# Moving fourteen subtractions from GpSimd to VectorE in a fused attention and Mish kernel, with a new written order for its four blocks

## The chip, the cores and the metric

One core of a Trainium2 chip runs the kernel in one launch. The metric is device time in microseconds (us); the time before is the median of three runs. A core has TensorE (PE in the profile: matrix products into PSUM), VectorE (DVE), ScalarE (ACT), GpSimd (POOL), and a queue on SyncE (SP) from which nearly all DMAs of this kernel are issued, in order. The engines run on their own and wait for each other through semaphores.

## The reference, cut to what matters

Two branches read the same `x` of 2048 x 512 and a gate mixes them.

```
qkv = x @ wqkv                              # 32 heads of 16
pq, pk = q @ w_phi[h], k @ w_phi[h]
phi = concat(softmax(p), softmax(-p))       # for q and for k: 32 features a head
kv  = phi_k^T v ;  z = sum_s phi_k
o   = (phi_q kv) / (phi_q z + 1e-6)
a   = o @ wo
h   = x @ w1 + b1                           # 512 -> 1376
act = h * tanh(log(1 + exp(h)))             # Mish
b   = act @ w2
g   = sigmoid(sum(x * gate_w))
out = g * a + (1 - g) * b
```

## The kernel before

**Two phases.** Phase A goes over 8 chunks of 256 rows (keys `("A", c)`) and makes keys, values, `phi_k^T v`, `z` and the queries' projection `pq`, which goes to DRAM as `pqd`. Phase B goes over 4 blocks of 512 rows, B0 to B3 (keys `("B", b)`). Each block does the Mish branch for its rows, and the softmax work of the queries, `num` (`phi_q kv`) and the product with `wo`. All matmuls run on fp32r operands: an fp32 value is split into a high part (`act(h, x)`, a copy on ScalarE that rounds) and a low part (`l = x - h`, a subtraction on VectorE or GpSimd), and a product is three matmuls (h*h, h*l, l*h). So each operand made on the way costs a copy and a subtraction.

**The order is written by hand.** Each piece of work is a named step, put in a table by `at(key, name, fn)`. `run` walks a text of names and calls them; `'`, `"` and `+` after a name mean the previous block, the one before that, and the next block. Each engine's queue holds the instructions in the order in which the text calls them (`tc.keep_in_program_order`), and SP's DMAs too. BLOCK0 to BLOCK3 are these texts; from B1 on they are built from `pairs(g, ...)`, g = 0 to 3, and `end(...)`.

**Steps of the softmax work, for tile t of 4 (128 rows each) of a block.** `lq` loads `pq` by SP. `mx`, `mn` (VectorE, maximum and minimum per head), `d0`, `d1` (VectorE, the differences for the two signs, into `E`), `E` (ScalarE, Exp), `S` (sum per head), `T` (`E` times `z`), `rS` (reciprocal), `D` (sum of T), `m`, `de`, `rd`, `sc` (small ones on 32 or 64 columns), `es` (`E` times the scale), `tr` (a transpose on VectorE, then an SP DMA to a DRAM tile `ed`). `mv0` and `mv1` are four SP DMAs each, which bring `ed` of tiles 0 and 1, or 2 and 3, back as `eT`. `nu0` and `nu1` are 32 small matmuls each from `eT` into two PSUM banks `num`; `oh` (ScalarE) and `ol` (VectorE) split them into `ohl`, of which there are two buffers in all; `wo0` to `wo3` are 12 matmuls each, `wo0` and `wo1` from `nu0`, `wo2` and `wo3` from `nu1`. `ag` (ScalarE) scales `wo` by the gate into `io`, `fi` (VectorE) adds the Mish branch and sends the tile out. `ge` and `gg` make the gate; `gr` and `gl` move its row through DRAM.

**Steps of the Mish branch.** B0 has 11 column groups: `up` (12 matmuls), `mi` (ScalarE, Mish), `hi` (ScalarE), `lo` (GpSimd, the low part), `dn` (12 matmuls). B1 to B3 have one such group, and five pairs of groups that share seven products of 6 matmuls of 256 columns. Within `pairs(g, ...)` TensorE runs `s3_g`, then `s1` of the next pair, `s4_g`, a `dn`, `s2` of the next pair and a `dn`. VectorE adds partial sums in `a1`, `a2`, `a3` (line 787); `s4_g` overwrites what `a3_g` reads. ScalarE copies in `c1`, `c2` and does Mish in `M0`, `M1` and the high parts in `H0`, `H1`; GpSimd makes the low parts in `L0`, `L1` (line 806). `wa` and `wb` load weight sums (`wA`, `wB`) from a DRAM tile `prod`.

**Steps that prepare the next block.** `LX0`, `LX1` load `xraw` by SP. `XH0`, `XH1` (ScalarE) and `XL0`, `XL1` (line 567; VectorE for B0, GpSimd for the others) make the parts of `x`; `TT0` to `TT3` (VectorE, lines 584 to 588) make differences, which `TH0`, `TH1` (ScalarE) and `TL0`, `TL1` (GpSimd, line 601) split. `ls`, `hs`, `os`, `ts` (line 493 is `os`) load weight sums, split them and send them to `prod`; `ldo`, `WH`, `WL` (line 627 is `WL`) do so with `wo`, and `wh0`, `wl0` in B0 with the last piece of `w2b` (line 437 is `wl`).

ScalarE holds one table of functions at a time. Exp and Mish are in different ones; a load stands in its queue wherever the next function needs the other.

Of the kernel before, what the change touches and what calls it, by code (L numbers as in the profile page):

```python
# [107 lines left out]
BLOCK3 = (
    """
    up0 mi0 S0 T0 s1_0 wb_0 c1_0 hi0 a1_0 lo0 gr df2' fi2' df3' fi3' gl s2_0 c2_0 a2_0 M0_0 H0_0 L0_0 hc rS0 D0 m0 de0 rd0 sc0 dn0  # L110
    """
    + pairs(0, "es0", "tr0 S1 T1", "rS1 D1 m1 de1 rd1 sc1")
    + pairs(1, "es1", "tr1 mv0 S2 T2", "rS2 D2 m2 de2 rd2 sc2")
    + pairs(2, "es2", "tr2 S3 T3", "ge rS3 D3 m3 de3 rd3 sc3")
    + pairs(3, "es3", "gg tr3 mv1", "cd nu0 oh0 ol0")
    + """
    s3_4 wa_4 a3_4 wo0 ag0 s4_4 wb_5 M1_4 H1_4 L1_4 wo1 ag1 nu1 oh1 ol1 df0 fi0 df1 fi1 wo2 ag2 wo3 ag3 mo df2 fi2 df3 fi3
    """
# [4 lines left out]
def tile_gated_mix(ctx: ExitStack, tc: tile.TileContext, xT, wv, wkT, wqT, bd, w1a, w1b, b1, w2a, w2b, wo, out):  # L123
# [328 lines left out]
    def sum_ops():  # L452
# [25 lines left out]
        for g in range(NFB):  # L478
# [10 lines left out]
            def hs(d=d):  # L489
                act(d["h"], f32(d["l"]))  # L490

            def os(d=d):
                pin(G_.tensor_sub(d["l"], f32(d["l"]), f32(d["h"])))
# [58 lines left out]
    def x_ops(b, load, split):  # L552

        raw = {}
        for h in range(2):
# [8 lines left out]

            def xl(h=h):
                sl = slice(h * SC, (h + 1) * SC)
                pin((G_ if b else V).tensor_sub(xb[b][1][:, :, sl], kt(raw[h], SC), f32(xb[b][0][:, :, sl])))
# [587 lines left out]
```

## Time and profile before

| | |
|---|---|
| median of three runs (459.22 to 463.14) | 460.75 us |
| time of the profiled execution | 464.13 us |
| its span, first to last instruction | 462.4 us |
| phase A on TensorE | until about 150 us |
| B0, up to the first matmul of B1 | 150 to 237.94 us |
| B1 | 237.94 to 308.88 us |
| B2 | 308.88 to 385.96 us |
| B3 and the end | 385.96 to 462.4 us |
| busy: TensorE, VectorE, ScalarE, GpSimd | 96%, 77%, 49%, 45% |

The profile is one execution. Its views are: the page (shares, the span in 40 slices, the costliest groups), the waits of an engine (who waited for whom), the timeline of an engine (start, length, engine, line, operation, output and inputs; in brackets the idle time before it and what ended that), windows (busy time in a stretch) and groups by line. "SPq" rows are DMA issues on SyncE's queue. A matmul's length in the timeline overlaps its successor's; the distance of their starts is what it takes. Lines are those of the kernel before.

### The profile page before, as it was taken

Reading aid. Unit: us, or ns where it says so; the run is one execution under the profiler, and the core shown is the slowest. Engines: PE = TensorE matmul, PEld = TensorE weight load, DVE = VectorE, ACT = ScalarE, POOL = GpSimd, SP = SyncE. Lnnn points to the kernel's source line nnn. Section 1 sums busy time; section 2 is a strip of 40 time slices with the busy share of each in tenths; the row PEclk is TensorE's granted clock in tenths of the full one; section 3 lists DMA queues with packets and bytes.
Section 4 is the critical chain, followed back from the end, with each engine's and each line's share of the span. In section 5 each row is a group of like instructions: output and inputs, shape, how many; then the busy total and the mean of one; then the engine's idle time right before and its main releaser. Section 6 shows DMA issues by size and latency. Waiting matters only on the chain.

```text
span 462.4 us, 7984 instructions
## 1 busy us (share of the span) xinstructions
PE 443.3 (96%) x3144; PEld 371.7 (80%) x3144; DVE 354.1 (77%) x471; ACT 228.5 (49%) x355; POOL 206.6 (45%) x121
## 2 busy tenths in 40 slices
PE   8999999999999989996699999999999969999997
PEld 7888888888888868783488988878899748888876
DVE  3996937858799999996985897646897588899522
ACT  3644434434425356554538634488333668544631
POOL 3078795896364274551743422462222182222210
PEclk9999999999999999998889999999999989999999
DMA  8721989998531348819849967715889831867512
GB/s 257 268 92 50 324 241 231 257 349 278 176 119 64 86 121 322 229 52 317 315 183 296 368 258 233 307 45 190 291 229 321 239 123 55 286 221 219 196 49 92
DMA packets 53214, 96.50 MB, mean 209 GB/s; under 512 B 6836, under 2 KB 27828, under 8 KB 53176
## 3 DMA queue, kind: packets, MB, share of 16 engines
q1 hardware_dynamic: 51640, 91.00, 58.6%
q0 software_dynamic: 1248, 4.59, 5.2%
q8 instruction: 25, 0.41, 0.4%
q10 hardware_dynamic: 288, 0.39, 0.3%
q14 instruction: 13, 0.11, 0.1%
HBM read 69.35 MB, written 33.17 MB: 222 GB/s over the span
## 4 chain that ended last, share of the span: by engine, by line
PE 35%; DVE 22%; DMA 6%; ACT 4%; issue 2%; SPq 0%; POOL 0%; DVEq 0%; ACTq 0%
PE down L134 15%; PE upa L134 7%; PE wo L134 7%; PE upb L134 5%; DMA xraw<-in_xT_dram 3%; DVE E L320 2%; DVE T L873 2%; DVE Dn L877 2%; DVE E L303 2%; DVE Sm L309 1%; DVE xt L588 1%; DMA ed<-E 1%; PE up L134 1%; DVE xt L584 1%; DVE E L888 1%
## 5 line engine op out<-in xcount | busy, mean ns | idle before, releaser
L806 POOL TENSOR_TENSOR l<-act,h 128x512 fp32r<-128x512 f32 x30 | 40.8, 1359 | 121.0 <-ACT h L154 84.7
L363 POOL TENSOR_TENSOR zacc<-zacc,E 128x1024 f32<-128x1024 f32 x16 | 39.6, 2477 | 34.5 <-DVE E L320 24.8
L134 PE MATMUL wo<-woh,ohl 128*128 128x512 f32 x128 | 44.7, 417 | 8.1 <-ACT ohl L154 7.9
L154 ACT ACTIVATE E<-E 128x1024 f32<-128x1024 f32 x32 | 33.3, 1058 | 37.8 <-DVE E L305 37.7
L320 DVE TENSOR_TENSOR E<-E,Sm 128x1024 f32<-128x1024 f32 x32 | 48.9, 1530 | 0.7
L309 DVE TENSOR_REDUCE Sm<-E 128x64 f32<-128x1024 f32 x32 | 38.5, 1202 | 1.7 <-ACT E L154 1.7
L716 POOL TENSOR_TENSOR l<-act,h 128x512 fp32r<-128x512 f32 (+1 forms) x14 | 19.4, 1392 | 45.0 <-ACT h L154 20.3
L134 PEld LDWEIGHTS wo<-woh,ohl 128*128 128x128 f32 x128 | 26.0, 203 | 15.0 <-ACT ohl L154 8.7
L134 PE MATMUL down<-w2ah,h 128*128 128x512 f32 x95 | 37.3, 392 | 0.0
L787 DVE TENSOR_TENSOR act<-upb,act 128x256 f32<-128x256 f32 x30 | 12.6, 421 | 28.1 <-ACT act L154 18.9
L134 PE MATMUL down<-w2ah,l 128*128 128x512 f32 x79 | 31.0, 392 | 1.6 <-POOL l L716 1.6
L134 PE MATMUL down<-w2bh,h 128*128 128x512 f32 x79 | 32.1, 407 | 0.0
L154 ACT ACTIVATE h<-act 128x512 fp32r<-128x512 f32 (+2 forms) x48 | 30.3, 632 | 3.1 <-ACT act L154 0.7
L134 PE MATMUL down<-w2bl,h 128*128 128x512 f32 x79 | 31.4, 398 | 0.0
L134 PE MATMUL down<-w2bh,l 128*128 128x512 f32 x79 | 31.0, 393 | 0.0
L134 PE MATMUL down<-w2al,h 128*128 128x512 f32 x79 | 30.9, 392 | 0.0
L289 DVE TENSOR_REDUCE mx<-proj 128x32 f32<-128x512 f32 x16 | 11.0, 689 | 25.3 <-PE proj L134 25.3
L281 POOL TENSOR_TENSOR xl<-xraw,xh 128x512 fp32r<-128x512 f32 x14 | 20.4, 1601 | 18.6 <-ACT xh L154 18.6
L931 DVE TENSOR_TENSOR ohl<-num,ohl 128x512 fp32r<-128x512 f32 x16 | 10.4, 686 | 21.7 <-ACT ohl L154 18.7
L134 PE MATMUL wo<-wol,ohl 128*128 128x512 f32 x64 | 26.8, 419 | 0.0
L154 ACT ACTIVATE qs<-proj 128x512 f32<-128x512 f32 x16 | 9.6, 599 | 33.4 <-PE proj L134 29.1
L154 ACT ACTIVATE act<-act,b1s 128x512 f32<-128x512 f32 (+1 forms) x30 | 18.4, 614 | 13.9 <-DVE act L787 13.8
(170 smaller groups left out, 1202.2 us busy)
## 6 DMA issues: line engine op xcount, KB each, us to landing
wA<-prod SPq DMA_DIRECT2D x15, 1024.0 KB, 5.8
wB<-prod SPq DMA_DIRECT2D x15, 768.0 KB, 5.7
ed<-E SPq DMA_DIRECT2D x16, 512.0 KB, 4.5
eT<-ed SPq DMA_DIRECT2D x32, 256.0 KB, 4.7
xraw<-in_xT_dram SPq DMA_DIRECT2D x15, 512.0 KB, 7.7
...
```

Source lines behind the costliest of these rows:

```text
L134: return pin(nc.tensor.matmul(*a, **k))
L154: return pin(A_.activation(out_, in_, fn, **k))
L281: pin(eng.tensor_sub(xs[c][1][j], kt(rawx[c], SC)[:, 2 * j : 2 * j + 2, :], f32(xs[c][0][j])))
L289: pin(V.tensor_reduce(d[name], hv(src()), axis=AX.X, op=op))
L303: pin(V.tensor_sub(E, hv(src()), d["mx"][:, :, None].to_broadcast([P, H, DH])))
L309: pin(V.tensor_reduce(d["S"], hv(d["E"][:, :]), axis=AX.X, op=ALU.add))
L320: pin(eng.tensor_mul(hv(d["E"][:, :]), hv(d["E"][:, :]), d["S"][:, :, None].to_broadcast([P, 2 * H, DH])))
L363: at(key, f"z{t}", lambda d=d: pin(G_.tensor_add(zacc, zacc, d["E"])))
L716: pin(G_.tensor_sub(U[i]["l"][:n, :], U[i]["a"][:n, :], f32(U[i]["h"][:n, :])))
L787: pin(V.tensor_add(o, ps, o))
L806: pin(G_.tensor_sub(u["l"], d["A"][j], f32(u["h"][:, :])))
L931: pin(V.tensor_sub(ohl[h, gp][:, 512:], num[h, gp], f32(ohl[h, gp][:, :512])))
```

## The change

Fourteen low parts that GpSimd made are made by VectorE: `wl0` in B0, `os` of all five groups, `WL0` and `WL1`, and `XL0`, `XL1` of B1, B2 and B3. GpSimd keeps `lo`, `L0`, `L1`, `TL0`, `TL1`.

In B0 the whole softmax work of B1's tile 0 and most of tile 1's (`S` to `tr`) leaves the end of the block; only `mx` to `E` of both tiles and `S0`, `T0`, `rS0` stay. In B1 and B2, `mx` to `E` of the next block's tiles 2 and 3 leave the end, except `mx2` and `mn2`, and are done within the next block's pairs 0 and 1. `D0` to `tr0` come after `a3_0`. `nu0` comes before `dn8` in B0, and `nu1` behind `dn9`. `LX0`, `LX1` stand behind `mv1` in each block. In `end`, `oh1` and `ol1` stand ahead of `TT2`, `TT3`, `TH0`, and `XL1` ahead of `TT0`. In B0, `ls2` and the `ts` steps are issued at other places. The step `pm` puts the load of Mish's table directly behind the Exps.

```diff
-    up0 lq3 mi0 gr gl hi0 lo0 ldo0 ldo1 S1 rS1 up1 up2 mi1 hi1 lo1 hs0 os0 wh0 wl0 d02 d12 T0 D0 m0 de0 rd0 sc0 es0 tr0 mi2 hi2 ts0 up3 dn0 hc lo2 hs1 os1
-    mi3 hi3 lo3 T1 D1 m1 de1 rd1 sc1 es1 tr1 ts1 mv0 lq0+ lq1+ mx3 mn3 d03 d13 WH0 dn1
-    up4 mi4 hi4 lo4 WH1 WL0 dn2 E2 S2 T2 rS2 D2 m2 de2 rd2 sc2 es2 tr2 up5 mi5 hi5 lo5 WL1 dn3 E3 ge gg up6 mi6 hi6 lo6 ls2 dn4
-    up7 mi7 hi7 lo7 dn5 S3 T3 rS3 D3 m3 de3 rd3 sc3 es3 tr3 mv1 hs2 os2 up8 mi8 hi8 lo8 dn6
-    mx0+ mn0+ d00+ d10+ mx1+ mn1+ d01+ d11+ lq2+ lq3+ ts2 up9 mi9 hi9 lo9 dn7 E0+ E1+ S0+ T0+ LX0 rS0+ D0+ LX1 m0+ de0+ rd0+ sc0+
-    up10 mi10 hi10 lo10 dn8 dn9 cd nu0 nu1 ls3 wi oh0 XH0+ XH1+ XL0+ XL1+ ol0 TT0+ TT1+ TT2+ TT3+ es0+ tr0+ TH0+ TL0+ TH1+ TL1+ S1+ df0 df1 wo0 ag0
-    wo1 oh1 ol1 T1+ rS1+ ag1 D1+ fi0 m1+ de1+ rd1+ sc1+ hs3 os3 df2 wo2 ag2 fi1 es1+ wo3 ag3 ts3 tr1+ ls4+
+    up0 lq3 mi0 gr gl hi0 lo0 ldo0 ldo1 S1 rS1 up1 up2 mi1 hi1 lo1 wh0 wl0 hs0 d02 d12 T0 D0 m0 de0 rd0 sc0 es0 tr0 mi2 hi2 os0 up3 dn0 hc lo2 hs1
+    mi3 hi3 lo3 T1 D1 m1 de1 rd1 sc1 es1 tr1 ts0 os1 mv0 lq0+ lq1+ mx3 mn3 d03 d13 WH0 dn1
+    up4 mi4 hi4 lo4 WH1 WL0 WL1 ls2 ts1 dn2 E2 pm S2 T2 rS2 D2 m2 de2 rd2 sc2 es2 tr2 up5 mi5 hi5 lo5 dn3 E3 ge pm gg up6 mi6 hi6 lo6 dn4
+    up7 mi7 hi7 lo7 hs2 os2 ts2 dn5 S3 T3 rS3 D3 m3 de3 rd3 sc3 es3 tr3 mv1 up8 mi8 hi8 lo8 dn6
+    mx0+ mn0+ d00+ d10+ mx1+ mn1+ d01+ d11+ lq2+ lq3+ up9 mi9 hi9 lo9 dn7 LX0 LX1
+    up10 mi10 hi10 lo10 E0+ E1+ pm nu0 dn8 oh0 ol0 cd dn9 nu1 ls3 wi XH0+ XH1+ XL0+ XL1+ TT0+ TT1+ df0 df1 wo0 ag0
+    wo1 oh1 ol1 TT2+ TT3+ ag1 TH0+ TL0+ TH1+ TL1+ fi0 hs3 os3 df2 wo2 ag2 fi1 S0+ T0+ rS0+ wo3 ag3 ts3 ls4+
...
-def end(f3, last):
+def end(f3, last, tail):
...
-    s3_4 wa_4 a3_4 wo0 ag0 {f3} s4_4 wb_5 M1_4 H1_4 L1_4 dn9 XH0+ XH1+ XL0+ XL1+ TT0+ TT1+ TT2+ TT3+ wo1 ag1 TH0+ TL0+ nu1 oh1 ol1 TH1+ TL1+ {last} df0 df1 wo2 ag2 wo3 ag3 fi0 fi1
+    s3_4 wa_4 a3_4 wo0 ag0 {f3} s4_4 wb_5 M1_4 H1_4 L1_4 dn9 XH0+ XH1+ XL0+ d01+ d11+ XL1+ TT0+ TT1+ wo1 ag1 nu1 oh1 ol1 TT2+ TT3+ TH0+ TL0+ {tail} TH1+ TL1+ pm {last} df0 df1 wo2 ag2 wo3 ag3 fi0 fi1
...
 BLOCK1 = (
-    up0 mi0 mx2 mn2 hi0 s1_0 wb_0 c1_0 gr a1_0 lo0 mv0 gl fi2' df3' fi3' d02 d12 s2_0 c2_0 a2_0 M0_0 H0_0 L0_0 mx3 mn3 hc dn0
+    up0 mi0 s1_0 wb_0 c1_0 hi0 a1_0 lo0 gr gl fi2' df3' fi3' s2_0 c2_0 a2_0 M0_0 H0_0 L0_0 hc dn0
...
-    + pairs(0, "d03 d13", "lq0+ lq1+ lq2+", "hs4 os4 S2 T2 rS2", "E2 E3 ge")
-    + pairs(1, "D2 m2 de2 rd2 sc2", "es2 tr2", "ts4 S3 T3 rS3 gg")
-    + pairs(2, "D3 m3 de3 rd3 sc3", "es3 tr3 mv1", "mx0+ mn0+ d00+ d10+ lq3+")
-    + pairs(3, "mx1+ mn1+ LX0 LX1", "d01+ d11+ mx2+ mn2+", "cd nu0 oh0 ol0 d02+ d12+")
-    + end("mx3+ mn3+ d03+ d13+", "E0+ E1+ E2+ E3+")
+    + pairs(0, "D0 m0 de0 rd0 sc0", "es0 tr0 mx2 mn2", "os4 d02 d12", "hs4")
+    + pairs(1, "mx3 mn3 d03 d13", "S1 T1 rS1 D1", "m1 de1 rd1 sc1 es1 ts4", "E2 E3 ge pm")
+    + pairs(2, "tr1 mv0", "S2 T2 rS2 D2", "m2 de2 rd2 sc2 es2 tr2 lq0+ lq1+ lq2+")
+    + pairs(3, "S3 T3 rS3", "D3 m3 de3 rd3 sc3 es3 tr3 mv1 LX0 LX1", "mx0+ mn0+ cd nu0 oh0 ol0 gg")
+    + end("d00+ d10+ mx1+ mn1+ lq3+", "mx2+ mn2+", "E0+ E1+")
 BLOCK2 = (
-    up0 mi0 S0 T0 s1_0 wb_0 c1_0 hi0 a1_0 lo0 gr df2' fi2' df3' fi3' gl s2_0 c2_0 a2_0 M0_0 H0_0 L0_0 hc rS0 D0 m0 de0 rd0 sc0 dn0
+    up0 mi0 S0 T0 s1_0 wb_0 c1_0 hi0 a1_0 lo0 gr df2' fi2' df3' fi3' gl s2_0 c2_0 a2_0 M0_0 H0_0 L0_0 hc rS0 dn0
...
-    + pairs(0, "es0", "tr0 S1 T1", "rS1 D1 m1 de1 rd1 sc1 lq0+ lq1+ lq2+")
-    + pairs(1, "es1", "tr1 mv0 S2 T2", "rS2 D2 m2 de2 rd2 sc2")
-    + pairs(2, "es2", "tr2 S3 T3", "rS3 D3 m3 de3 rd3 sc3")
-    + pairs(3, "es3", "tr3 mv1 mx0+ mn0+ LX0 LX1", "d00+ d10+ cd nu0 oh0 ol0 lq3+ ge gg")
-    + end("mx1+ mn1+ d01+ d11+", "mx2+ mn2+ d02+ d12+ mx3+ mn3+ d03+ d13+ E0+ E1+ E2+ E3+")
+    + pairs(0, "D0 m0 de0 rd0 sc0", "es0 tr0 d02 d12", "mx3 mn3 d03 d13")
+    + pairs(1, "S1 T1 rS1", "D1 m1 de1 rd1 sc1 es1 tr1", "", "E2 E3 ge pm")
+    + pairs(2, "mv0 S2 T2", "rS2 D2 m2 de2 rd2 sc2 es2", "lq0+ lq1+ lq2+ tr2 S3 T3")
+    + pairs(3, "rS3 D3 m3 de3 rd3 sc3", "es3 tr3 mv1 LX0 LX1", "mx0+ mn0+ cd nu0 oh0 ol0 gg")
+    + end("d00+ d10+ mx1+ mn1+ lq3+", "mx2+ mn2+", "E0+ E1+")
```

BLOCK3 changes as BLOCK2 does, without what it would prepare for a next block. The rest of the change:

```diff
     def run(text, key, prev=None, nxt=None, prev2=None):
         for w in text.split():
...
+            if w == "pm":
+                pin(A_.preload_act_table_set("mish"))
...
-                pin(G_.tensor_sub(l[:, o : o + n], r, f32(h[:, o : o + n])))
+                pin((V if c == NCH - 1 else G_).tensor_sub(l[:, o : o + n], r, f32(h[:, o : o + n])))
...
-            def os(d=d):
-                pin(G_.tensor_sub(d["l"], f32(d["l"]), f32(d["h"])))
+            def os(d=d, g=g):
+                pin((V if g == 2 else V).tensor_sub(d["l"], f32(d["l"]), f32(d["h"])))
...
-                pin((G_ if b else V).tensor_sub(xb[b][1][:, :, sl], kt(raw[h], SC), f32(xb[b][0][:, :, sl])))
+                pin((V if b else V).tensor_sub(xb[b][1][:, :, sl], kt(raw[h], SC), f32(xb[b][0][:, :, sl])))
...
-            pin(G_.tensor_sub(wob["l"][:, sl], raw[j], f32(wob["h"][:, sl])))
+            pin(V.tensor_sub(wob["l"][:, sl], raw[j], f32(wob["h"][:, sl])))
```

More of the change, by code (lines that the diff above doesn't have):

```diff
@@ L109 @@
     """
-    up0 mi0 S0 T0 s1_0 wb_0 c1_0 hi0 a1_0 lo0 gr df2' fi2' df3' fi3' gl s2_0 c2_0 a2_0 M0_0 H0_0 L0_0 hc rS0 D0 m0 de0 rd0 sc0 dn0
+    up0 mi0 S0 T0 s1_0 wb_0 c1_0 hi0 a1_0 lo0 gr df2' fi2' df3' fi3' gl s2_0 c2_0 a2_0 M0_0 H0_0 L0_0 hc rS0 dn0
     """
[L112 to L115, printed above, removed]
+    + pairs(0, "D0 m0 de0 rd0 sc0", "es0 tr0 d02 d12", "mx3 mn3 d03 d13")
+    + pairs(1, "S1 T1 rS1", "D1 m1 de1 rd1 sc1 es1 tr1", "", "E2 E3 ge pm")
+    + pairs(2, "mv0 S2 T2", "rS2 D2 m2 de2 rd2 sc2 es2", "tr2 S3 T3")
+    + pairs(3, "rS3 D3 m3 de3 rd3 sc3", "es3 tr3 mv1", "cd nu0 oh0 ol0 gg")
     + """
```

## The prediction

> **What bounds the kernel now.** I read the page first, then TensorE's waits, then its timeline row by row, then windows of VectorE's load. Nothing before about 150 us changes for TensorE, so the question is where it loses time in B0 to B3.
>
> ```profile
> span 462.4 us, 7984 instructions
> PE wo L134 <- ACT ohl L154: 7.9, 2, 4.4
> PE num L134 <- DMA eT<-ed: 3.9, 2, 3.3
> PE down L134 <- POOL l L716: 1.6, 1, 1.6
> PE upa L134 <- DVE act L787: 1.0, 3, 0.4
> ...
> 170.35 0.50 PE L134 MATMUL down<-w2ah,l 128*128 128x512 f32 x1 [1.62 <-POOL l L716]
> 170.68 0.39 PE L134 MATMUL down<-w2ah,h 128*128 128x512 f32 x1
> ...
> 214.48 1.56 PE L134 MATMUL num<-eT,kvb 64*32 64x256 f32 x30 [0.67 <-DMA eT<-ed]
> 215.97 0.80 PE L134 MATMUL down<-w2bh,h 128*128 128x512 f32 x1
> ...
> 229.66 0.79 PE L134 MATMUL wo<-woh,ohl 128*128 128x512 f32 x1 [4.36 <-ACT ohl L154]
> ...
> 237.94 1.98 PE L134 MATMUL up<-xbh,w1x 128*128 128x512 f32 x8
> ...
> 308.88 1.98 PE L134 MATMUL up<-xbh,w1x 128*128 128x512 f32 x8
> ...
> 318.88 0.40 PE L134 MATMUL upa<-xtl,wB 128*128 128x256 f32 x2
> ...
> 378.80 0.80 PE L134 MATMUL wo<-woh,ohl 128*128 128x512 f32 x1 [3.53 <-ACT ohl L154]
> ...
> 385.96 1.98 PE L134 MATMUL up<-xbh,w1x 128*128 128x512 f32 x8
> ...
> 303.60 5.44 PE wo L134 x24
> ...
> 205.00:238.00 33.00, 24.55 (x142) 17.46 (x141) 28.46 (x36) 13.91 (x17) 15.55 (x6) 0.84 0.70 255
> ```
>
> In the waits the columns are the total, the count and the longest. The losses are few and named: 14.4 us in eight places, of which `wo2` waiting for `oh1` takes 7.9 (229.66 in B0, 378.80 in B2) and `nu1` in B0 3.9. Behind the long ones the matmuls also get longer (0.80 at 215.97 against 0.39 at 170.68, which follows a wait of 1.62), and the window 205 to 238 has a granted clock of 0.84. At full speed 24 such matmuls take 5.44, so 0.227 each. B1 lasts 70.94 (308.88 − 237.94) and B2 77.08 (385.96 − 308.88): B1 has only waits of 0.4 and is nearly the floor, B2 is not.
>
> **B0 up to dn5.** The wait at 170.35 is for `lo2`, which stands behind other work on GpSimd; that work is lighter now, so 1.6 could go. But the stall comes back:
>
> ```profile
> 179.26 1.06 ACT L154 ACTIVATE woh<-raw 128x1024 fp32r<-128x1024 f32 x1 [1.99 <-DMA raw<-in_wo_dram]
> ...
> 185.51 1.29 POOL L716 TENSOR_TENSOR l<-act,h 128x512 fp32r<-128x512 f32 x1 [4.43 <-ACT h L154]
> ...
> 186.07 0.93 SPq L869 DMA_DIRECT2D pq<-pqd  x2
> ```
>
> `WH1` waits on ScalarE for a transfer until 179.26, and SP's order up to it is unchanged. Behind it stand `E2` with two table loads, `mi5` and `hi5`, so `lo5` ends at 186.80 as before (185.51 + 1.29), and TensorE, 1.6 us ahead, waits there instead. Gain 0; bounds 0 and 1.6.
>
> **The end of B0.** Here the change does most.
>
> ```profile
> 191.11 0.64 ACT L154 ACTIVATE h<-act 128x512 fp32r<-128x512 f32 x1
> 192.87 0.59 SPq L487 DMA_DIRECT2D sl<-sums  x1
> 193.89 1.21 DVE L309 TENSOR_REDUCE Sm<-E 128x64 f32<-128x1024 f32 x1
> 197.38 1.06 ACT L154 ACTIVATE sh<-sl 128x1024 fp32r<-128x1024 f32 x1 [5.63 <-DMA sl<-sums]
> 198.51 2.41 POOL L493 TENSOR_TENSOR sl<-sl,sh 128x1024 fp32r<-128x1024 f32 x1 [4.97 <-ACT sh L154]
> 198.69 2.32 DVE L885 TENSOR_TENSOR Sm<-Sm,den 128x64 f32<-128x64 f32 x1
> 201.04 2.21 DVE L320 TENSOR_TENSOR E<-E,Sm 128x1024 f32<-128x1024 f32 x1
> 203.29 1.25 DVE L888 STREAM_TRANSPOSE E<-E 128x1024 f32<-128x1024 f32 x1
> 214.94 0.23 DVE L885 TENSOR_TENSOR Sm<-Sm,den 128x64 f32<-128x64 f32 x1
> ```
>
> `nu1` needs `tr3`, which ended at 204.54 (203.29 + 1.25). Two VectorE rows ahead of it overlap GpSimd's `os2` (198.51 to 200.92): 2.32 where the same line takes 0.23 undisturbed, and 2.21 where the sum over a tile of that size takes 1.21, so 3.1 too much. The Trainium skill (page "SBUF — State Buffer", section "Who interferes with whom") says that a two-input VectorE instruction and a GpSimd one exclude each other for the whole instruction; the row of 2.32 under one of 2.41 agrees, and it speaks against a full VectorE too, because `L0`, `L1` and `TL` stay on GpSimd; its price is in rival D.
>
> After: `ls2` goes out behind the `pq` issues (186.07 + 0.93 = 187.0) and, at the old distance of 4.5 (197.38 − 192.87), is there at 191.5; `hs2` starts behind `hi7` (191.75), `os2` on VectorE ends about 194, so `S3` starts at 193.9 as before (193.89), and without the overlaps, though with one of the head's small rows disturbed by `lo8`, `tr3` ends at 202.6 instead of 204.54: 1.9 earlier. Its way through DRAM to `nu1` took 11.43 (215.97, the first `df` matmul behind `nu1`, less 204.54) and keeps that: 214.0. `LX0` and `LX1` now go out behind it, before `E0` of B1, and the softmax work of B1 is gone from VectorE.
>
> Behind it come, in both orders, `df0`, `df1`, `df2` and `wo0` to `wo3` as 57 matmuls: 12.9 at 0.227. The `nu1` wait itself shrinks to about 2, as `dn8` and `nu0` now stand in front. The clock is the open part: 3.9 of waiting left slow matmuls behind it (0.80), 1.62 did not (0.39). I charge half of the 2.2 us that the slow stretch behind `nu1` cost: 1.0, since 2 lies between these ends. So B1 starts at 214.0 + 12.9 + 1.0 = 227.9, and B0 gains 237.94 − 227.9 = 10.0.
>
> The Trainium skill (page "TensorE: Matmul & The Clock Gate", section "What's actually happening") has the clock fall to half after an idle window of about 3.4 us; by that the gap of 2 costs nothing and the result is 1.0 lower (452.0); the 3.9 with slow matmuls and the 1.62 without agree with it.
>
> For 10.0 to hold, `wo2` may not wait at about 221.5. Before, it waited because `oh1` stood behind `TH0`:
>
> ```profile
> 220.50 5.19 POOL L567 TENSOR_TENSOR xbl<-xraw,xbh 128x1024 fp32r<-128x1024 f32 x2 [6.04 <-ACT xbh L154]
> ...
> 146.89 1.21 DVE L567 TENSOR_TENSOR xbl<-xraw,xbh 128x1024 fp32r<-128x1024 f32 x1
> ```
>
> `TH0` needs `TT0`, `TT1`, and these were disturbed by the two `XL` on GpSimd (5.19). `XL` on VectorE costs 1.21 each, as in the row of B0's own, and `oh1` now stands ahead of `TH0`. It starts when `wo1` frees its buffer (220.8), and `ol1` ends near 223.1 against a need at 223.3. So the cover is exactly used up; if it fails by 4 us, the gain falls to 6.0. Bounds of this term: 6.0 and 12 (both stalls and the slow stretch gone).
>
> **B1.** Its work up to `tr3` is what the block before left over. The windows of three full pairs give VectorE's load:
>
> ```profile
> 318.40:328.90 10.50, 10.08 (x64) 9.03 (x63) 9.89 (x14) 5.61 (x14) 2.58 (x2) 1.00 0.86 277
> 328.90:339.40 10.50, 10.50 (x67) 9.52 (x66) 8.88 (x14) 4.21 (x9) 2.64 (x2) 1.00 0.84 285
> 339.40:350.60 11.20, 11.20 (x70) 10.10 (x70) 10.09 (x15) 4.12 (x9) 3.03 (x3) 1.00 0.83 261
> ...
> 356.27 0.67 DVE L289 TENSOR_REDUCE mn<-pq 128x32 f32<-128x512 f32 x1
> ```
>
> The third busy time (9.89, 8.88, 10.09) is VectorE's: mean 9.62 for one tile's `S` to `tr`, three partial sums and the collisions. Four tiles: 38.5. Off go `S0`, `T0`, `rS0`, done earlier (1.21 + 1.2 + 0.3 = 2.7), and 0.3 of small things; added are `mx`, `mn`, `d0`, `d1` of tiles 2 and 3, eight rows of some 0.6 from start to start (the row at 356.27 is one; 4.8), and `os4` (1.2). Sum 41.5. It starts when the first pair's third product ends, 10.2 into a block (318.88 + 0.24 − 308.88), since `D0` now stands behind `a3_0`. So `tr3` ends 51.7 into B1. In B2 before it ended at 46.9:
>
> ```profile
> 354.55 1.23 DVE L888 STREAM_TRANSPOSE E<-E 128x1024 f32<-128x1024 f32 x1
> ...
> 371.44 1.06 ACT L154 ACTIVATE xbh<-xraw 128x1024 fp32r<-128x1024 f32 x1 [0.16 <-DMA xraw<-in_xT_dram]
> 372.70 0.69 ACT L154 ACTIVATE io<-wo,g_sb 128x512 f32<-128x512 f32 x1 [0.20 <-PE wo L134]
> ...
> 378.17 1.07 ACT L154 ACTIVATE ohl<-num 128x512 fp32r<-128x512 f32 x2
> ```
>
> That is the term I like least. SP works in order, and in B1 `LX0`, `LX1` stand behind `mv1`, which waits for `tr3` (before too, but there `tr3` and `mv1` were in pair 2 and `LX` in pair 3; now `tr3` is in pair 3 itself). Queued behind the waiting `mv1` are `LX`, so `XH1` on ScalarE, and behind `XH1` in ScalarE's order `ag1` and `oh1`, which `wo2` needs. From `tr3` to `XH1` B2 took 15.66 (371.44 − 355.78); then 1.06 for `XH1`, 0.69 for `ag1`, 0.53 for the first half of `oh1`: 18.0. So `wo2` starts at 51.7 + 18.0 = 69.7, where TensorE is ready at 65.5 (70.94 − 5.44). The idle time of 4.2 is like those of 4.36 and 3.53, which were followed by slow matmuls: another 1.64. With `wo2`, `wo3` (5.44), B1 lasts 69.7 + 1.64 + 5.44 = 76.8: a loss of 5.8 against 70.94. Bounds: a loss of 0.7 (`LX` in time) and of 8.8 (three us more on VectorE).
>
> **B2.** The same with no `os4` and with two rows fewer: 39.0 (38.5 − 2.7 + 6 × 0.6 − 0.4), `tr3` at 49.3, `oh1` at 67.3: 1.8 late, too little for a slow stretch. Behind `wo3` I add 1.25, because `ol1` now stands behind `XL1`, `TT0`, `TT1` on VectorE. 67.3 + 5.44 + 1.25 = 74.0, a gain of 3.1 against 77.08, where `oh1` stood behind `TH0` (378.17) and the two disturbed `TT`. Bounds 0 and 5.5 (nothing late, 71.6).
>
> **B3** has no next block to prepare, and its `nu1` data go out ahead of where `LX` stood; with `a3_0` ahead of `D0` one wait of the 1.0 in three goes: gain 0.5, bounds 0 and 0.6.
>
> ```profile
> 311.84 1.28 ACT L154 ACT_TABLE_LOAD   x1 [0.89 <-PE up L134]
> ```
>
> **Mish's table** by `pm`: the load at 311.84 (1.28) moves ahead of the block's start, where ScalarE is idle; loads are as many as before. It stood beside TensorE's `up0` anyway: 0. If its cover were gone it would cost 1.28 in each of three blocks.
>
> **The sum.** 10.0 − 5.8 + 3.1 + 0.5 = 7.8. The profiled execution took 464.13 (its span 462.4 and 1.73 around it): 456.3. The median of the runs shown, 460.75, is 3.4 lower than the profiled one: 453.0 (own range 448 to 457).
>
> **The rivals.**
>
> B, the transfers come in time. If VectorE, freed of GpSimd's disturbance, ends `tr3` of B1 at 46.9 too, both blocks take 71.6: B1 loses 0.7, B2 gains 5.5. Total 10.0 − 0.7 + 5.5 + 0.5 = 15.3, so 445.5. For it: fewer GpSimd rows and so fewer like the 2.32. Against it: the windows are already at 9 to 10 busy of 10.5, and more is added. Chance 0.23.
>
> C, the gain of B0 is given back in B0: `ol1` misses its 0.2 of cover and the clock stays low, so 6.0 instead of 10.0. Total 3.8: 457.0. For it: the 0.84 over the whole stretch. Chance 0.18.
>
> D, slower: VectorE becomes the bound in B1 to B3. Place: `s4` of each pair, which waits for `a3` (`upa` in the waits, 0.4 now). The work that left B0's end and 1.21 per low part are added to lists of 9.62. From 10.5 a pair on, plus some 2 us of matmuls of the next `s1` as cover, each further us is paid on TensorE. At 1 us each in 12 pairs: 12. 10.0 − 5.8 + 3.1 − 12 = −4.7: 465.5. Against it: before, the same lists cost only 0.4 in three places. Chance 0.14.
>
> E, the change doesn't do what it says: ScalarE's order or the DRAM trip decides anyway, and each wait comes back under another name, as I argue for `lo5`: 460.75. Chance 0.07.
>
> **How the numbers follow.** Main 0.38, B 0.23, C 0.18, D 0.14, E 0.07. A difference of about 1% can be told from none: below 456.1 is faster, above 465.4 slower. Faster: most of the main case (0.33), B, and 0.03 of C, 0.59. Slower: about 0.10 of D (its term can be above 1 us), with 0.05 for `pm` uncovered or B1 at its bound on top of C: 0.15. Same: 0.26. Range: 443 leaves out the lower part of B, 462 most of D, together 0.2.
>
> **What would show it.** Right: `up` of B1 starts near 228, no row of `ohl` waits at B0's `wo2`, `S` to `tr` rows of VectorE at 1.2 without 2.2 in B0; B1's `wo2` shows a wait of 4 us for `ohl` or `xraw`, B2's under 2. Wrong: `upa` waits of 1 us in every pair (D), a `wo2` in B1 without any wait (B), a wait above 3 at `nu1` or `wo2` in B0 (C).

## The result, and the profile after

| | before | after |
|---|---|---|
| median of 13 runs each | 460.94 us (458.72 to 464.99) | 456.68 us (454.35 to 458.31) |
| ratio | | 0.9899, 95% interval 0.9869 to 0.9928 |
| profiled execution | 464.13 us, span 462.4 | 457.17 us, span 455.3 |

The kernel became 1.0% faster, 4.3 us; 7.8 had been forecast (453.0 us). The two profiled executions differ by 6.96. Read block by block from the first `up` of each (columns: start, length in us, engine, line, operation, output and inputs), they answer the forecast's terms:

```profile
span 455.3 us, 7982 instructions
...
228.92 1.98 PE L134 MATMUL up<-xbh,w1x 128*128 128x512 f32 x8
...
306.77 1.98 PE L134 MATMUL up<-xbh,w1x 128*128 128x512 f32 x8
...
379.15 1.98 PE L134 MATMUL up<-xbh,w1x 128*128 128x512 f32 x8
```

| | before | after | gain | forecast |
|---|---|---|---|---|
| B0 and what lies ahead of it, to B1's `up` | 237.94 | 228.92 | 9.0 | 10.0 |
| B1 | 70.94 | 77.85 | −6.9 | −5.8 |
| B2 | 77.08 | 72.38 | 4.7 | 3.1 |
| B3 and the end of the span | 76.44 | 76.15 | 0.3 | 0.5 |
| sum | | | 7.1 | 7.8 |

TensorE's waits after (total, count, longest) and the rows behind them:

```profile
PE num L134 <- DMA eT<-ed: 3.5, 2, 2.7
PE upa L134 <- DMA wB<-prod: 2.9, 1, 2.9
PE wo L134 <- ACT ohl L154: 2.0, 1, 2.0
PE wo L134 <- DVE ohl L933: 2.0, 2, 1.1
...
185.73 0.50 PE L134 MATMUL down<-w2ah,l 128*128 128x512 f32 x1 [0.63 <-POOL l L718]
...
212.00 0.59 PE L134 MATMUL num<-eT,kvb 64*32 64x256 f32 x2 [2.75 <-DMA eT<-ed]
213.34 1.96 PE L134 MATMUL num<-eT,kvb 64*32 64x256 f32 x30 [0.75 <-DMA eT<-ed]
215.23 0.79 PE L134 MATMUL down<-w2bh,h 128*128 128x512 f32 x1
...
216.63 0.40 PE L134 MATMUL down<-w2bh,h 128*128 128x512 f32 x1
...
279.13 0.71 PE L134 MATMUL upa<-xth,wB 128*128 128x256 f32 x4 [2.95 <-DMA wB<-prod]
...
299.70 0.50 PE L134 MATMUL wo<-woh,ohl 128*128 128x512 f32 x1 [2.04 <-ACT ohl L154]
...
302.86 1.56 PE L134 MATMUL wo<-woh,ohl 128*128 128x512 f32 x5 [1.06 <-DVE ohl L933]
...
375.25 1.56 PE L134 MATMUL wo<-woh,ohl 128*128 128x512 f32 x5 [0.94 <-DVE ohl L933]
```

Of B0's gain of 9.0, 5.9 are idle time of TensorE (10.1 before, 4.1 after) and 3.1 busy time (78.0, 74.9), which is fewer slow matmuls (granted clock in the block 0.94, then 0.98); of B2's 4.7, 3.0 and 1.7. B0's wait at `wo2` (4.36) and B2's (3.53) are gone, and no wait of `upa` for VectorE is left. What is left in B0 is `nu1` (2.75 and 0.75) with matmuls that are slow until 216.63. B1 has three waits it did not have: for `wB` (2.95), for `oh1` (2.04) and for `ol1` (1.06). B1's two chains, from VectorE's last transpose, over SP's queue, to ScalarE:

```profile
262.93 0.34 SPq L893 DMA_DIRECT2D ed<-E  x1
269.90 1.81 SPq L913 DMA_DIRECT2D eT<-ed  x4
271.75 0.53 SPq L527 DMA_DIRECT2D wB<-prod  x1
...
278.86 1.25 DVE L890 STREAM_TRANSPOSE E<-E 128x1024 f32<-128x1024 f32 x1
280.13 0.33 SPq L893 DMA_DIRECT2D ed<-E  x1
287.88 2.47 SPq L913 DMA_DIRECT2D eT<-ed  x4
290.39 0.92 SPq L560 DMA_DIRECT2D xraw<-in_xT_dram  x2
297.53 1.06 ACT L154 ACTIVATE xbh<-xraw 128x1024 fp32r<-128x1024 f32 x1 [0.25 <-DMA xraw<-in_xT_dram]
299.06 1.08 ACT L154 ACTIVATE ohl<-num 128x512 fp32r<-128x512 f32 x2
```

The upper three rows: SP issued `tr1`'s `ed` at 262.93 and then stood 7.0 us at `mv0`, which needs that `ed` back from DRAM; `wB`, queued behind it, went out at 271.75 and landed when TensorE had been waiting for 2.95. The lower six: the same with `tr3`, `mv1`, and `LX` behind it, up to `oh1`.

### The profile page after: what moved, and what is told of

Same layout as the page of the kernel before. It is cut to its first block, busy times and chain, and to the rows that moved or that the text cites. A ratio compares the mean times of both kernels' runs of the same rounds, so it can differ in the third digit from the quotient of the medians.

```text
span 455.3 us, 7982 instructions
## 1 busy us (share of the span) xinstructions
PE 439.3 (96%) x3144; PEld 367.9 (81%) x3144; DVE 349.4 (77%) x485; ACT 229.1 (50%) x355; POOL 170.3 (37%) x107
## 4 chain that ended last, share of the span: by engine, by line
PE 77%; DMA 10%; DVE 7%; SPq 2%; issue 2%; ACT 1%; POOL 1%; POOLq 0%; ACTq 0%
PE proj L134 28%; PE down L134 18%; PE upa L134 8%; PE upb L134 7%; PE wo L134 7%; PE up L134 6%; DMA ed<-E 2%; DMA wA<-prod 2%; PE kvp L134 2%; DMA sl<-sums 2%; DMA wT<-in_wkT_dram 1%; DMA xraw<-in_xT_dram 1%; DMA eT<-ed 1%; SPq L913 1%; PE num L134 1%
## 5 line engine op out<-in xcount | busy, mean ns | idle before, releaser
L322 DVE TENSOR_TENSOR E<-E,Sm 128x1024 f32<-128x1024 f32 x32 | 45.6, 1425 | 0.9
L134 PE MATMUL wo<-woh,ohl 128*128 128x512 f32 x128 | 41.9, 394 | 4.0 <-ACT ohl L154 2.0
L718 POOL TENSOR_TENSOR l<-act,h 128x512 fp32r<-128x512 f32 (+1 forms) x14 | 18.1, 1293 | 49.1 <-ACT h L154 38.9
L603 POOL TENSOR_TENSOR xtl<-xt,xth 128x1024 fp32r<-128x1024 f32 x6 | 16.5, 2762 | 43.5 <-ACT xth L154 43.5
L134 PEld LDWEIGHTS wo<-woh,ohl 128*128 128x128 f32 x128 | 23.7, 188 | 10.5 <-DVE ohl L933 3.5
L154 ACT ACTIVATE act<-upa 128x256 f32<-128x256 f32 x30 | 11.5, 385 | 27.4 <-PE upa L134 27.3
L134 PE MATMUL wo<-wol,ohl 128*128 128x512 f32 x64 | 25.0, 390 | 0.0
```

The lines of the kernel that those rows point to most:

```text
L134: return pin(nc.tensor.matmul(*a, **k))
L154: return pin(A_.activation(out_, in_, fn, **k))
L322: pin(eng.tensor_mul(hv(d["E"][:, :]), hv(d["E"][:, :]), d["S"][:, :, None].to_broadcast([P, 2 * H, DH])))
L603: pin(G_.tensor_sub(raw["l"][:, pair(j)], raw["t"][:, pair(j)], f32(raw["h"][:, pair(j)])))
L718: pin(G_.tensor_sub(U[i]["l"][:n, :], U[i]["a"][:n, :], f32(U[i]["h"][:n, :])))
```

## The experiments

The lengths of the blocks in each profiled execution, in us, beside the medians. The ratio is to the kernel before, timed again beside each run (medians of 460.9 to 461.3). A profiled execution need not be a middling one: of its kernel's runs that of e5 and that of e9 were the fastest, e8's was the slowest, e6's the second fastest of twelve.

| | B0 | B1 | B2 | B3 | median | ratio to before (95%) |
|---|---|---|---|---|---|---|
| before | 88.1 | 70.9 | 77.1 | 76.4 | 460.9 | |
| before, second profile (e1) | 87.1 | 71.0 | 77.7 | 76.7 | | |
| after | 79.0 | 77.9 | 72.4 | 76.2 | 456.7 | 0.9899 (0.9869 to 0.9928) |
| e2 LX ahead | 78.5 | 76.5 | 71.0 | 75.8 | 452.2 | 0.9804 (0.9770 to 0.9838) |
| e3 mv0 later | 78.9 | 76.1 | 72.4 | 76.0 | 452.9 | 0.9823 (0.9778 to 0.9867) |
| e4 both | 77.7 | 75.2 | 71.0 | 75.8 | 451.0 | 0.9790 (0.9749 to 0.9830) |
| e5 moves alone | 86.9 | 74.7 | 73.4 | 78.0 | 465.5 | 1.0121 (1.0087 to 1.0155) |
| e6 order alone | 79.7 | 78.6 | 72.8 | 75.8 | 461.2 | 0.9994 (0.9964 to 1.0024) |
| e7 oh1 back | 79.3 | 80.8 | 77.6 | 76.0 | 464.4 | 1.0075 (1.0045 to 1.0105) |
| e8 no early table | 81.0 | 79.6 | 72.9 | 75.8 | 458.3 | 0.9931 (0.9906 to 0.9955) |
| e9 all three | 73.0 | 73.3 | 71.0 | 75.7 | 447.4 | 0.9690 (0.9644 to 0.9735) |
| e10 moves, repaired | 83.3 | 72.0 | 73.4 | 78.2 | 458.5 | 0.9945 (0.9917 to 0.9974) |
| e11 LX between | 73.6 | 73.2 | 71.1 | 76.0 | 445.1 | 0.9641 (0.9600 to 0.9683) |
| e12 B0 both back | 80.0 | 75.4 | 71.9 | 76.0 | 454.6 | 0.9855 (0.9806 to 0.9905) |

**The kernel before, profiled again.** No edit.

> The kernel before, unchanged, profiled a second time. The first profiled execution took 464.13 us, 3.2 above the median of 460.94; the one of the kernel after 457.17, 0.5 above its median of 456.68. Theory S (the excess sits in the stalls that the change removes): in an execution near 461, phase A and B1 are as long as in the first profile (within 0.5 us) and B0 (87.9) or B2 (77.1) are together 2 to 3 us shorter, with shorter waits or a higher granted clock behind them. Rival (the excess is spread over the whole execution, so that it may be subtracted as one constant): every stretch is shorter by its share, 0.7%, about 1 us of it in phase A.

It took 463.72, so the comparison with an execution near 461, which the expectation wanted, was not to be had. B0 came out 1.0 shorter and B2 0.6 longer, phase A 0.3 shorter: single executions move the stalled blocks by such amounts, and both profiled ones of this kernel lay some 3 above its median.

**B1's chain.** e2, e3 and e4 change where SP issues two steps:

```
e2, B1:  D3 m3 de3 rd3 sc3 es3 tr3 mv1 LX0 LX1  ->  D3 LX0 LX1 m3 de3 rd3 sc3 es3 tr3 mv1
e2, B2:  es3 tr3 mv1 LX0 LX1                    ->  LX0 LX1 es3 tr3 mv1
e3, B1:  "tr1 mv0", "S2 T2 rS2 D2", "m2 ..."    ->  "tr1", "S2 T2 rS2 D2", "mv0 m2 ..."
```

> The kernel after, with LX0 and LX1 of B1 and B2 issued directly behind D3 (B1) and ahead of es3 (B2), so ahead of mv1 on SP. Theory C (B1's loss ends at the chain tr3, mv1, LX, XH1, oh1): XH1 no longer waits, wo2 of B1 starts without its wait of 2.04 and without the 1.06 for ol1, B2 without its 0.94; B1 74.7, B2 71.4, total 4.0 less than after: about 452.7 us. Rival V (VectorE's full list decides through tr3 and the trip of eT, whatever LX does): nu1 or wo2 waits in the same place, B1 stays at 77 to 78, total 456 to 457. Rival W (mv0's stall of SP's queue and the late wB are the loss): no change either, and e3 gains 2.9.

> The kernel after, with mv0 of B1 moved from the first to the third place of pair 2, so that wB of that pair is issued ahead of it on SP. Theory C: the wait of 2.95 for wB goes, and wo2 waits 2.9 longer (4.9 instead of 2.04), since oh1 is set by tr3 and LX: 456.7 within 0.7, or up to 1.6 more if the clock falls behind the longer wait. Rival W (the late wB is the loss): 2.9 less, 453.8.

> Both edits of e2 and e3. Theory C: with the chain cut, the 2.95 of wB counts, up to the point where nu1 waits for eT (lands about 293 to 294 in the profile after, TensorE would be there at 291.8): 1 to 1.5 less than e2, about 451.4 us. Rival W: as e3, 453.8. Rival V: 456 to 457.

e2 gave 452.2, where theory C had 452.7, and its waits at `wo2` and for `ol1` are gone in both blocks; B2 is at 71.0. But B1 kept 76.5, where C had 74.7, because `nu1` now waits and `wB` still does (1.74). With `LX` issued 4.0 ahead of `tr3`'s `ed`, the way from `ed` to `mv1` took 10.67 (279.06 to 289.73), not 7.75 as in after. So B1 and B2 together gained 2.8 in the profile, not C's 4.0, and that the total came out as forecast is partly luck: B0 and phase A, which the edit does not touch, were 1.1 shorter. TensorE's rows of e2 and, below, of e4 in B1:

```profile
295.38 0.59 PE L134 MATMUL num<-eT,kvb 64*32 64x256 f32 x2 [2.81 <-DMA eT<-ed]
296.40 1.09 PE L134 MATMUL num<-eT,kvb 64*32 64x256 f32 x30 [0.43 <-DMA eT<-ed]
297.42 0.50 PE L134 MATMUL down<-w2bh,h 128*128 128x512 f32 x1
297.76 0.40 PE L134 MATMUL down<-w2bl,h 128*128 128x512 f32 x1
```
```profile
292.19 0.59 PE L134 MATMUL num<-eT,kvb 64*32 64x256 f32 x2 [1.78 <-DMA eT<-ed]
293.21 1.38 PE L134 MATMUL num<-eT,kvb 64*32 64x256 f32 x30 [0.43 <-DMA eT<-ed]
294.52 0.79 PE L134 MATMUL down<-w2bh,h 128*128 128x512 f32 x1
295.11 0.63 PE L134 MATMUL down<-w2bl,h 128*128 128x512 f32 x1
```

e3 went against theory C: 452.9, where C had 456.7 and rival W 453.8. Its SP queue and wait:

```profile
262.57 0.52 SPq L527 DMA_DIRECT2D wB<-prod  x1
269.02 2.94 SPq L913 DMA_DIRECT2D eT<-ed  x4
...
278.72 0.33 SPq L893 DMA_DIRECT2D ed<-E  x1
285.57 1.81 SPq L913 DMA_DIRECT2D eT<-ed  x4
...
PE wo L134 <- ACT ohl L154: 1.8, 1, 1.8
```

`wB` goes out 9.2 earlier (262.57 for 271.75; B1 began 0.8 earlier) and the wait of 2.95 is gone, as both theories had it. `wo2` should by C have waited 4.9; it waits 1.8. The chain behind `tr3` moved too: `ed` to `mv1` takes 6.85 (285.57 − 278.72) instead of 7.75. So C was right on what `wo2` waits for (the row still names `oh1`) and wrong in taking the chain's length as fixed. That the transfers were less in each other's way is argued from these rows, not shown. B1 became only 1.8 shorter, although TensorE's idle time in it fell from 6.1 to 2.7: its busy time rose from 71.8 to 73.4, since from 297.78, behind the wait of 1.78, it ran slow matmuls (0.63 each, 0.39 ahead of it). e4 has both gains in part: B1 75.2, 451.0; the intervals of e2, e3 and e4 overlap.

Over all profiles in the new order the two causes are plain. In the six that keep `mv0`'s place, TensorE waits 0.9 to 3.1 for `wB` in B1, in the four that move it (e3, e4, e9, e11) not at all. In the six that keep `LX` behind `mv1`, `wo2` of B1 waits 1.4 to 2.0 for `oh1` (6.4 in e7, which moves `oh1`), in the four that issue `LX` ahead of `mv1` (e2, e4, e9, e11) not at all.

**Moves and order apart.** e5 is the kernel before with the fourteen moves alone, e6 the kernel after with the fourteen back on GpSimd.

```diff
 e5, on before:
-pin((G_ if b else V).tensor_sub(xb[b][1] ...      # and os, WL, wl of the last chunk
+pin((V if b else V).tensor_sub(xb[b][1] ...
 e6, on after: the reverse
```

> The kernel before in its old order, with the fourteen low parts on VectorE and nothing else changed. Theory M (the gain of B0 and B2 is the collision of GpSimd's rows with VectorE's): tr3 of B0 1.9 earlier, the two xt rows of 2.7 shrink to 0.7 and oh1 comes about 3 us earlier in B0 and 2 in B2, XL takes 1.21 each; B0 82 to 84 (87 to 88 before), B2 74 to 75.5 (77 before), B1 within 0.7 of 70.9; total 5 to 8 less: about 454.5 us. Rival O (the order is what gains, and the moves alone only fill VectorE): 459 to 461, and e6 keeps the gain.

> The kernel after in its new order, with the fourteen low parts back on GpSimd. Theory M: os2 on GpSimd makes tr3 of B0 1.5 to 2 later; XL on GpSimd makes TT0 and TT1 2.7 each again, and ol1, which stands behind them on VectorE, comes 3 to 4 us later in B0, B1 and B2: 7 to 10 more than after, 464 to 467 us, so slower than the kernel before. Rival O: within 2 of after, 456 to 458.

Neither theory had it. The moves alone made the kernel 1.2% slower, the order alone changed nothing that can be told, and both together gained 1.0%. The waits of TensorE in e5, with the VectorE rows that end them:

```profile
PE wo L134 <- DVE ohl L931: 4.6, 1, 4.6
PE upa L134 <- DVE act L787: 3.9, 3, 2.7
...
218.91 2.46 DVE L567 TENSOR_TENSOR xbl<-xraw,xbh 128x1024 fp32r<-128x1024 f32 x2 [3.05 <-ACT xbh L154]
221.29 1.28 DVE L931 TENSOR_TENSOR ohl<-num,ohl 128x512 fp32r<-128x512 f32 x2
...
258.14 1.46 DVE L493 TENSOR_TENSOR sl<-sl,sh 128x1024 fp32r<-128x1024 f32 x1 [3.29 <-ACT sh L154]
```

The `xt` rows were at 0.7 in e5, as forecast, and `wo2` of B0 had no wait. But in the old text `ol0` stands behind `XL0`, `XL1`. On GpSimd they did not hold it; on VectorE they do, and they wait for `LX`'s data: `wo0` of B0 waits 4.6. In B1 `a3` stands behind `os4`, which waits 3.29 for ScalarE. In e6 `os2` on GpSimd raises B0's wait at `nu1` to 4.42, 0.9 more than after's two, about half of the 1.5 to 2 expected; `XL` there costs B1 and B2 together under 1.2, not 6 or more. The profiled execution of e6 shows 0.8 of the 4.5 by which its median lies above after's; where the rest is, it does not show. In the same way the spans of e5's profile and before's are equal (462.5 and 462.4), since the one is the fastest of its six runs and the other lies 3 above its median: that e5 is slower rests on the medians, and its profile shows only where it loses and gains. B3, 1.6 longer in e5 and 1.8 in e10, is not explained.

e10 repairs these two places in e5:

```diff
-    ... wi oh0 XH0+ XH1+ XL0+ XL1+ ol0 TT0+ ...
+    ... wi oh0 ol0 XH0+ XH1+ XL0+ XL1+ TT0+ ...
-    V.tensor_sub(d["l"] ...                  # os
+    (G_ if g == 4 else V).tensor_sub(d["l"] ...
```

> As e5 (old order, low parts on VectorE), with two repairs: ol0 of B0 ahead of XL0 and XL1, and os4 of B1 back on GpSimd. Theory Q (the moves alone lost because VectorE's list is kept in order: in B0 ol0 stood behind XL, which waits for LX's data, 4.95 at wo0; in B1 a3 behind os4, which waits for ScalarE's hs4, 2.84): both waits go, B0 82 to 83 instead of 86.9, B1 71 to 71.5 instead of 74.7, B2 and B3 as in e5: 457 to 458.5 us. Rival (VectorE is full as such): the waits come back under a3 or ol, 463 to 466.

458.5, with B0 at 83.3 (86.9) and B1 at 72.0 (74.7): both waits are gone, though `wo2` of B0 now waits 2.48 for `oh1`. For `ol0`, which only changed places, the cause was the place in VectorE's order and not VectorE's load; for `os4`, which left VectorE, the two are not told apart.

**oh1's place.** e7 puts `oh1`, `ol1` back behind `TH0` in all three ends; e12 does so in B0 alone and puts B1's `XL` back on GpSimd:

```diff
 e7 and e12, B0:
-    wo1 oh1 ol1 TT2+ TT3+ ag1 TH0+ TL0+ TH1+ TL1+ fi0
+    wo1 TT2+ TT3+ TH0+ TL0+ TH1+ TL1+ oh1 ol1 ag1 fi0
 e7, end():
-    XL1+ TT0+ TT1+ wo1 ag1 nu1 oh1 ol1 TT2+ TT3+ TH0+ TL0+
+    XL1+ TT0+ TT1+ TT2+ TT3+ wo1 ag1 TH0+ TL0+ nu1 oh1 ol1
 e12 also:
-pin((V if b else V).tensor_sub(xb[b][1] ...
+pin((G_ if b == 1 else V).tensor_sub(xb[b][1] ...
```

> The kernel after, with oh1 and ol1 put back behind TT2, TT3 and TH0 (B0: behind TH1 too) in B0, B1 and B2. Theory of the prediction: wo2 waits for oh1 behind TH0: in B0 ScalarE's rows before oh1 end about 3 us later and wo2 waits 2 to 3.5; in B1 oh1 comes 2.5 later (TT0 to TT1, TH0), in B2 2.5 later and wo2 waits 1.5 to 3: total 5 to 8 more than after, 462 to 465. Rival: with the xt rows at 0.7 TH0 is done before oh1's inputs are there, and the place of oh1 is worth under 2: 457 to 458.5.

> The kernel after, in B0 alone oh1 behind TH0 and TH1 as in the kernel before and XL of B1's x on GpSimd. e7 put back the first and e6 the second, and wo2 of B0 waited in neither. Theory E (either is enough: undisturbed xt rows make TH early, or oh1 does not stand behind it): with both back wo2 waits 2 to 4 again, B0 81 to 83 against 79.0: 459 to 461 us. Rival L (the earlier issue of LX is what does it): B0 stays at 79 to 80, 456.5 to 457.5.

e7 lost 7.7, in B1 (80.8) and B2 (77.6), in two waits:

```profile
PE wo L134 <- ACT ohl L154: 10.3, 2, 6.4
```

In B0 it cost 0.3. e12, a waits row and its second `XH` (in before it started at 220.62), then `TH` and the `wo2` of B0:

```profile
PE wo L134 <- ACT ohl L154: 3.0, 2, 1.5
...
215.38 1.06 ACT L154 ACTIVATE xbh<-xraw 128x1024 fp32r<-128x1024 f32 x1 [0.21 <-DMA xraw<-in_xT_dram]
...
221.03 2.26 ACT L154 ACTIVATE xth<-xt 128x1024 fp32r<-128x1024 f32 x2 [1.38 <-DVE xt L590]
...
223.83 0.50 PE L134 MATMUL wo<-woh,ohl 128*128 128x512 f32 x1 [1.51 <-ACT ohl L154]
```

With both put back `wo2` waits 1.5, not 4.36, and B0 is 80.0. So 1.5 of the 4.36 went twice over, by the place of `oh1` or by undisturbed `xt` rows, and 2.9 went without either. What is left on that chain is `LX`'s data, 5.2 earlier than before. The rows carry this through: `TT0` (220.78 before, 215.53) and `TH0` (226.28, 221.03) start 5.2 earlier too, `oh1` 5.8 (229.02, 223.19), and TensorE reaches `wo2` 3.0 earlier, so its wait is 2.9 shorter. That the data alone would have done it, as rival L has it, is argued from these rows; an edit of `LX` alone was not run. The 454.6 lies below after's median; its profile is shorter in B1, which the edit does not touch.

**The early table.** e8 drops `pm`.

```diff
-                pin(A_.preload_act_table_set("mish"))
+                pass
```

> The kernel after without pm: Mish's table is loaded where the first Mish needs it. The prediction priced pm at 0. Theory: the load of 1.28 goes back behind TensorE's first up of a block, and Mish of the block's first group is 1.28 later, which dn0 does not wait for: within 0.7 of after, 456 to 457.4. Rival: the wait of hi0 or M0 reaches TensorE in B0 (lo5, lo6) and in three blocks: 1.3 to 5 more, 458 to 461.

458.3, 1.6 above after; the two intervals overlap, so a worth of `pm` between 0 and some 3 us stays open. The profile, the slowest of its eleven runs, gives no wait that answers to it. B1 is 1.7 longer than after's with 0.3 less of waiting in it (5.8 against 6.1) and a granted clock of 0.98 against 1.00. B0 is 1.9 longer than after's, and its row-by-row difference is mostly this: the slow matmuls behind `nu1` last until 219.66, not 216.63.

```profile
213.35 1.95 PE L134 MATMUL num<-eT,kvb 64*32 64x256 f32 x30 [0.75 <-DMA eT<-ed]
215.24 0.79 PE L134 MATMUL down<-w2bh,h 128*128 128x512 f32 x1
...
219.66 0.40 PE L134 MATMUL wo<-woh,ohl 128*128 128x512 f32 x1
```

**A faster version.** e9 adds to e4 a new order of B0's end; e11 puts B1's `LX` between `tr3` and `mv1`:

```
after: E0+ E1+ pm nu0 dn8 oh0 ol0 cd dn9 nu1 ls3 wi XH0+ XH1+ XL0+ XL1+ TT0+ TT1+ df0 df1 wo0 ag0  wo1 oh1 ol1 TT2+ TT3+
e9:    nu0 oh0 ol0 E0+ E1+ pm dn8 cd dn9 ls3 wi df0 df1 wo0 ag0 nu1 XH0+ XL0+  wo1 oh1 ol1 XH1+ XL1+ TT0+ TT1+ TT2+ TT3+
e11, B1: ... es3 tr3 LX0 LX1 mv1
```

> The edits of e4 and, in B0, oh0 and ol0 ahead of B1's two Exps, and nu1 behind df0, df1, wo0, with XH1 behind oh1. Theory T (in B0 the time is lost where TensorE stands at nu1 with nothing else to do, 2.9 + 1.0, and in the slow matmuls behind it): nu1 is reached at 213.2, where eT has landed (213.3), no wait and no slow stretch; up of B1 starts about 5 earlier than after's 228.92, B1 and B2 as in e4: 446 us. Rival: oh1 comes late behind XH0 and wo2 waits 2 to 3 instead, or nu1's data come later because the DMAs are what is full: 449.5 to 451.

> As e9, but in B1 LX0 and LX1 stand between tr3 and mv1 (SP issues them while it would wait for tr3's ed to land). Theory of e4's rest (LX's 1 MB ahead of ed on the DMA engines delays ed and so eT; nu1 then waits 2.6): ed lands 1.5 earlier, nu1 waits about 1 less, XH1 is still in time: 0.5 to 1 less than e9. Rival: LX now delays eT by as much, or XH1 is late and wo2 waits: same as e9 or up to 1.5 more.

447.4 and 445.1, 3.1% and 3.6% under the kernel before, and both faster than after; their intervals overlap, so between LX ahead and LX between nothing is settled. The profiles give e11's theory no support: `nu1` of B1 waits 0.9 in e11 and 1.0 in e9, and B1 takes 73.2 and 73.3. The waits for `eT` that are left in e9, both in B1, and its `nu1` in B0:

```profile
PE num L134 <- DMA eT<-ed: 1.0, 2, 0.6
...
212.68 1.09 PE L134 MATMUL num<-eT,kvb 64*32 64x256 f32 x32
213.70 0.50 PE L134 MATMUL wo<-woh,ohl 128*128 128x512 f32 x1
```

`nu1` has `df0`, `df1` and `wo0` ahead of it, no wait, and matmuls at full speed behind it (0.50, then 0.40); B0 is 6.0 shorter than after's. Theory T held for B0 in this execution, the fastest of six (its granted clock is 1.000, that of the others 0.992 to 0.996). B1 is 1.9 shorter than e4's, which theory T did not have: its `nu1` waits 1.0, not 2.2, and no slow matmuls follow.

## Why the prediction was right or wrong

**The direction, and the loss inside the gain,** came out as forecast: B0 and B2 gain, B1 loses, and each term lies within its bounds. On the scale of the profiled execution the sum was 456.3 against 457.17. That it came so near is partly luck: the blocks missed by 1.0, 1.1 and 0.2 one way and by 1.6 the other.

**The step that failed is the last one,** "453.0", the shift from the profiled execution to the median. I took 3.4 off because the profile of before lay 3.4 above its median. The one of after lies 0.5 above its own. That offset is a draw: before's two profiles lay 3.2 and 2.6 above (medians of 460.94 and, for the runs beside e1, 461.09), e6's 3.2 below (457.94 for a median of 461.18). So 2.9 of the 3.7 by which 453.0 was too low is this, and 0.8 the blocks. What makes executions of one kernel scatter by up to 7 us is open in part. Stretches of slow matmuls have a share in it, as e8's profile against after's shows and as the mean granted clock of each execution says: of e9's six, the one at 1.000 took 444.4, three at 0.996 took 447.0 to 447.7, and two at 0.992 took 448.3 and 450.6. They are not all: after's executions at 0.992 lie between 454.4 and 456.7, and its two at 0.996 took 455.2 and 457.2.

**dn5.** "Gain 0" was wrong by 1.1: the stall came back under `lo5` as argued, but its matmul ran at 185.73, not 186.86, because the `wo` data and so `WH1` came earlier.

**B0's end.**

The first row is of the kernel before, the second of the one after:

```profile
200.87 3.53 POOL L716 TENSOR_TENSOR l<-act,h 128x512 fp32r<-128x512 f32 x2
...
201.77 1.25 DVE L890 STREAM_TRANSPOSE E<-E 128x1024 f32<-128x1024 f32 x1
```

`tr3` ended at 203.02 (202.6 forecast): `os2` was 1.3 late, since its transfer landed later, and `S3` to `tr3` was shorter, with the 2.32 and 2.21 rows gone. Only the first of these lay under `os2`, which ended at 200.92. The row of 2.21 began at 201.04, beside two `lo` rows that stood behind `os2` on GpSimd and stay there; after, it takes 1.22 because no `lo` row falls beside it.

From `tr3` to the end of `nu1` it took 12.21 (215.23 − 203.02), not 11.43, as `nu1`'s own 30 matmuls ran slow (1.96; in e2 1.09). The rest took 13.69 (228.92 − 215.23), where 12.9 and 1.0 were forecast; slow matmuls cost about 0.7 of it (six `df` in 2.10 for 1.36), and in before 1.4 behind `nu1` (2.75 for 1.36), not the 2.2 of which I took half. The wait at `nu1` was 3.5, not 2.

The low clock was charged 1.0 on the ground that a wait of 2 lies between 1.62 and 3.9 (which was 3.25 and 0.67). The stretch was there, but the ground was not: 2.81 and 0.43 left matmuls at 0.40 in e2, 1.78 and 0.43 left them at 0.63 in e4. The rule of the Trainium skill that I weighed (page "TensorE: Matmul & The Clock Gate", section "What's actually happening") also says that the window of some 3.4 us runs freely. These two pairs of rows agree with that part: the length of a wait alone does not decide. The reading "a gap of 2 costs nothing" is not tested in B0, where the gap was 3.5; in B1 of e4, where it was 2.2, the matmuls behind it took 0.79 and 0.63, so there it did not hold.

I put the end of the `wo2` wait to `oh1`'s place and to `XL`. By e12 these were worth 1.5 of its 4.36; the rest is most likely `LX` being issued and landing earlier, which the text mentions without a price. And "the cover is exactly used up" held: no wait.

**B1.** `tr3` at 51.7 was the best of the terms: 51.2 (278.86 + 1.25 − 228.92), with VectorE busy nearly throughout:

```profile
239.45:280.11 40.66, 37.71 (x239) 33.97 (x238) 38.40 (x57) 20.70 (x39) 11.32 (x8) 1.00 0.79 251
```

Third from the left is VectorE, 38.4 of 40.66. From `tr3` to `wo2` it took 19.6 (18.0 forecast). No slow stretch followed, where 1.64 was charged (by the rows of before that it was likened to, 24 matmuls of `wo` took 8.28 and 7.16 for 5.44, so 2.8 and 1.7). That the idle time was split, with 2.95 of it already at `wB`, may be why; it is not shown, and in e3 slow matmuls followed a single wait of 1.78. The wait at `wB` I did not foresee: I named what stands behind `mv1` on SP and not what stands behind `mv0`. Removing it gained, by e3. So B1's total came near by luck: 2.95 for `wB` and 1.06 for `ol1` were not foreseen, and 1.64 for the clock and half of the 4.2 at `wo2` did not come.

**B2.** `tr3` came 50.3 into the block (49.3 forecast), and yet `wo2` had no wait where I charged 1.8:

```profile
355.80 1.25 DVE L890 STREAM_TRANSPOSE E<-E 128x1024 f32<-128x1024 f32 x1
...
369.83 1.06 ACT L154 ACTIVATE xbh<-xraw 128x1024 fp32r<-128x1024 f32 x1 [0.16 <-DMA xraw<-in_xT_dram]
```

`XH1` started 12.8 after `tr3` (369.83 − 357.05), not 15.66. The 1.25 for `ol1` was 0.94. **B3** gave 0.3 for 0.5.

**The rivals.** B (transfers in time) did not hold, but e2 and e9 show it for B2, at 71.0, where I had 71.6. C did not: B0 kept its gain. D's mechanism was not seen after, no wait of `upa` for VectorE; e5 has it (3.9), and of that 2.7 went when e10 put `os4` back on GpSimd. E failed, though e6 and e5 show that each half of the change alone would have been E or worse.
